# An attention and expert kernel: equal experts first, fewer fill products, other orders

## The chip, the core and the metric

The kernel runs on one core of a Trainium2 chip. A core has TensorE (PE, matrix products; PEld is its weight load), VectorE (DVE), ScalarE (ACT), GpSimd (POOL) and SyncE (SP), each with its own instruction stream, and 16 DMA engines that all of them share. The metric is the device time of one execution in microseconds; lower is better.

## The reference

The attention has 8 batches of 8 heads, 576 positions, 64 columns per head and 32 memory slots. phi is turned into weights by a softmax over the slots, and k and v are averaged with them to 32 rows per head; q then attends to these 32 rows.

```python
a = exp(phi - max(phi, axis=2)); a = a / (sum(a, axis=2) + 1e-09)
k_m = einsum('bhsm,bhsd->bhmd', a, k); v_m = einsum('bhsm,bhsd->bhmd', a, v)
attn = softmax(q @ k_m.T / sqrt(64));  x = attn @ v_m      # then [4608, 512]
y_dense = relu(x @ w1_dense) @ w2_dense
expert_idx = argmax(x @ w_gate, axis=1);  gate_w = softmax(x @ w_gate)[expert_idx]
y_moe[mask] = gate_w[mask, None] * (relu(x[mask] @ w1[e]) @ w2[e])   # for each expert e of 8
out = y_dense + y_moe
```

All is float32 outside; the hidden width is 512.

## The kernel before

The work is done batch by batch. A place in the order, 0 to 7, is not the batch's number: `seq` says which batch of the input stands at each place, and all names below use the place (`k` of batch 1 is that of the second place). For each batch the kernel picks one expert for all its rows from an estimate (`choose`, from the mean weights of v), loads that expert's two weight matrices, and keeps a flag; rows that would have needed another expert are handled at the end by a general path (`others`) behind a branch, which these inputs do not enter.

The steps of a batch, with their names in the order string: loads `Lphi`, `Lk`, `Lv`, `Lq`; `e0`, `e1` exponentials of phi (L352); `z`, `rz` their sums; `kv` (at place 0 apart as `kk` and `vv`) the sums over positions (L392), with `km` and `vm` after them; `T` (`Tk`, `Tv`) transposes of the means; `vTc`, `kTc` copies; `qT0`, `qT1` transposes of q on DVE; `s` scores (L503); `ET0`, `ET1` exponentials; `Z0`, `Z1` their sums (L536); `ln0`, `ln1`, `inv0`, `inv1` the reciprocals on ACT; `A0`, `A1` the attention (L565); `vg`, `vgc`, `pc`, `choose` the expert (L573 to L616); `L`, `mxeq`, `ex`, `gates` the gate of each row. The dense half folds v's means into w1_dense (`fd`, then copies `vd0`, `vd1`), takes four hidden products `hd0` to `hd3` (L741) with their relu `Hd`, and five output chunks `yd0` to `yd4` (L818; `yd4` is the half-size last one) written to `y` by `Yd`. The expert half is the same with `fe`, `ve`, `he`, `He`, `ye`, and `Ye` adds it to `y` with the row's gate (L853). The last place (`INNER`) multiplies the gate in at `He` and has one sum for both halves.

Loads. k, v, q and all weights are cast from float32 to float16 by GpSimd's DMA queue (L221, L249, L255, L259, L271, L276); phi goes there too (L204), but for the first batch's, which SP loads in halves (L213). `w1` and `w2` of a batch (L271, L276) need the chosen expert in a register of GpSimd, which its queue waits for at that point, with all later loads behind it. There are four places for expert weights (`NW`, `place_of`). At a place in `PAIRED`, the load carries a condition and is skipped when the expert is that of the batch before. Stores `o0`, `o1` (two chunks together) and `o4` (the last one, in two halves) are issued by SP (L859, L870).

Order. Everything is in one written order, `ORDER`, which is walked once by `go`; each engine takes its own steps in that order. `/A`, `/V`, `/P` picks ScalarE, VectorE or GpSimd for a step, and `+n` puts n fill products (L181) ahead of a step's own products: products of a matrix of ones into the PSUM tile that the step writes next, which compute nothing that is used. The tail is a branch on `any_i` at L1002 around the general path; the program's last instructions have line L1032.

```python
n, waits[0] = waits[0], 0
for _ in range(n):
    nc.tensor.matmul(p, lhsT=onesb, rhs=onesb[:, 0:1].to_broadcast([128, p.shape[1]]), start=True, stop=True)
```

Of the kernel before, what the change touches and what calls it, by code (L numbers as in the profile page):

```python
# [25 lines left out]
Yd3:0/V Lq:1 w2:0 yd0:0 fd:1 qT0:1 vgc:1 Yd0:0/A pc:1+7 Lphi:2/P kTc:1/V Lv:2 Lk:2 qT1:1 s:1+3  # L26
ye0:0+1 ET0:1 Lq:2 ET1:1 Lv:3 Z0:1 ln0:1 vd1:1/V inv0:1 Lq:3 vd0:1/V ye3:0 Z1:1 ye4:0 ln1:1 choose:1
Ye0:0 inv1:1 Lphi:4/P Ye3:0 A0:1 yd2:0 ye2:0 A1:1 Yd2:0/A hd1:1 ye1:0 hd3:1 Ye2:0 L:1 Ye1:0 w1:1
mxeq:1 e1:2 e0:2 Hd1:1/A ex:1 hd0:1 Ye4:0 Hd0:1/A z:2 fe:1 ve0:1/A Hd3:1/V ve1:1/A kv:2 hd2:1 rz:2
vm:2 km:2 qT0:2 T:2+5 vTc:2/A w2:1 fd:2 Hd2:1/A yd4:1 Lphi:3/P kTc:2/A qT1:2 vd1:2/A vg:2 vd0:2/V  # L30
vgc:2 s:2 Yd4:1/A ET0:2 yd3:1 pc:2 choose:2 gates:1 Z0:2 ET1:2 ln0:2 Yd3:1/V yd2:1 he1:1 inv0:2 A0:2
He1:1/A Z1:2 yd0:1 ln1:2 qT0:3 inv1:2 he0:1 He0:1/A Lk:3 A1:2 Yd0:1/V he2:1 yd1:1 He2:1/A he3:1
He3:1/A hd3:2 L:2 ye0:1 Hd3:2/V mxeq:2 hd0:2 e0:4 Yd2:1/V Ye0:1 Hd0:2/V e0:3 hd1:2 qT1:3 ex:2 e1:3
ye2:1 z:3 kv:3 Hd1:2/A Yd1:1/A hd2:2 ye1:1 rz:3 km:3 vm:3 Ye2:1 T:3 Ye1:1 e1:4 Hd2:2/A yd4:2 Yd4:2/V
kTc:3/A s:3 w1:2 ye4:1 vTc:3/A Ye4:1 ET1:3 fe:2 ve0:2/V vg:3 Lv:4 Lq:4 vgc:3 Lk:4 w2:2 Z1:3 ET0:3
ve1:2/A ye3:1 ln1:3 inv1:3 he3:2 He3:2/V Z0:3 ln0:3 pc:3 yd0:2 inv0:3 yd1:2 Yd0:2/A he1:2 yd2:2
Yd1:2/A He1:2/A A1:3 choose:3 Ye3:1 A0:3 he2:2 L:3 He2:2/A he0:2 gates:2 fd:3 ex:3 kv:4 mxeq:3 z:4
He0:2/V Yd2:2/A qT1:4 yd3:2 rz:4 km:4 vm:4 vd0:3/A vd1:3/A hd1:3 Hd1:3/A qT0:4 ye1:2 T:4 ye3:2
Yd3:2/A Ye1:2 kTc:4/A s:4 ET1:4 w1:3 vTc:4/A Ye3:2 ye0:2 Ye0:2 ET0:4 fe:3 vg:4 Z1:4 ln1:4 Z0:4 vgc:4
pc:4 ve1:3/V ln0:4 ye2:2 choose:4 Ye2:2 ve0:3/A hd0:3 hd2:3 Hd0:3/A Hd2:3/V ye4:2 fd:4 Lphi:5/P  # L40
inv1:4 inv0:4 hd3:3 Hd3:3/A Ye4:2 vd1:4/A he1:3 Lk:5 yd2:3 he0:3 vd0:4/V A0:4 Lv:5 yd3:3 He1:3/A
# [995 lines left out]
```

## Time and profile before

| | us |
|---|---|
| median of 3 runs | 171.67 (169.57 to 172.39) |
| the profiled execution | 169.97 |
| its span, first to last instruction | 168.3 |
| PE busy in it | 148.2 (88%) |
| DVE busy | 109.1 (65%) |
| ACT busy | 93.1 (55%) |
| POOL busy | 33.6 (20%) |

The span is shorter than the execution by what lies around it, 1.67 us. Busy times are shares of the span; fill products count as busy. A busy PE includes products at either clock. The DMA engines are shared, and their share of busy time is a mean over 16.

### The profile page before, as it was taken

The page shows a single profiled execution, that of the slowest core. Times are in us where ns is not written, and L with a number is a line of the kernel's source. Part 1 is how long each engine was busy: PE and PEld are TensorE (multiplying, and loading weights), DVE is VectorE, ACT ScalarE, POOL GpSimd, SP SyncE. Part 2 cuts the span into 40 slices and gives each one's busy share as a digit, 9 for nine tenths or more (in the row PEclk, how much of TensorE's full clock was granted, in tenths as well). Part 3 has the DMA queues.
Part 4 walks back from the last instruction along what each step waited for, and adds up shares of the span by engine and source line. Part 5 has one row for each costly group of instructions (what it writes and reads, how often), then busy time and mean ns, then how long its engine had stood idle before and what let it go on. Part 6 is the DMA issues. An engine that isn't in the chain of part 4 may idle for free.

```text
span 168.3 us, 5081 instructions
## 1 busy us (share of the span) xinstructions
PE 148.2 (88%) x2133; PEld 86.9 (52%) x2133; DVE 109.1 (65%) x296; ACT 93.1 (55%) x204; POOL 33.6 (20%) x56
## 2 busy tenths in 40 slices
PE   7964989988998999999899979999996999999910
...
DMA  4999807999999999999999999999999999679650
GB/s 119 185 201 236 218 7 90 205 208 257 232 208 207 299 248 208 208 214 161 229 210 206 248 241 208 179 196 223 208 200 201 320 357 345 195 291 383 244 167 9
DMA packets 22549, 36.06 MB, mean 214 GB/s; under 512 B 1268, under 2 KB 18676, under 8 KB 22520
## 3 DMA queue, kind: packets, MB, share of 16 engines
...
## 4 chain that ended last, share of the span: by engine, by line
PE 55%; DMA 27%; DVE 6%; issue 5%; POOLq 2%; ACT 1%; POOL 1%; DVEq 0%; ACTq 0%
PE p_y L818 28%; DMA W<-in_moe_w_dram 16%; DMA kv<-in_k_dram 11%; PE p_h L741 10%; PE p_kv L392 3%; PE p_att L181 2%; PE p_s L181 2%; PE p_vw L721 2%; PE p_s L503 2%; PE p_z L536 1%; POOLq L623 1%; PE p_att L643 1%; DVE qT L480 1%; PE p_kv L181 1%; DVE y L853 1%
## 5 line engine op out<-in xcount | busy, mean ns | idle before, releaser
L818 PE MATMUL p_y<-W,HTe 128*128 128x512 f16 (+1 forms) x192 | 37.2, 345 | 2.0 <-DMA W<-in_moe_w_dram 1.9
L818 PE MATMUL p_y<-w2d,HTd 128*128 128x512 f16 (+1 forms) x192 | 37.3, 345 | 0.0
L853 DVE SCALAR_TENSOR_TENSOR y<-p_y,gm,y 128x512 f32<-128x512 f32 (+1 forms) x35 | 23.9, 693 | 9.3 <-PE p_y L818 8.8
L271 POOL DMA_DIRECT2D W<-in_moe_w_dram x8 | 4.6, 572 | 97.2 <-DMA W<-in_moe_w_dram 23.1
L818 PEld LDWEIGHTS <-HTe 128*128 128x128 f16 (+1 forms) x192 | 15.0, 101 | 14.4 <-DMA W<-in_moe_w_dram 2.5
L781 ACT ACTIVATE HTd<-p_h 128x576 f16<-128x576 f32 x21 | 13.7, 651 | 13.0 <-PE p_h L741 11.0
L844 ACT ACTIVATE y<-p_y 128x512 f32<-128x512 f32 (+1 forms) x25 | 13.5, 555 | 13.2 <-PE p_y L818 13.2
L818 PEld LDWEIGHTS <-HTd 128*128 128x128 f16 (+1 forms) x192 | 14.9, 101 | 11.4 <-issue 1.1
L741 PE MATMUL p_h<-A,vwd 128*128 128x288 f16 x128 | 20.6, 287 | 0.3 <-ACT HTd L781 0.2
L741 PE MATMUL p_h<-A,vwe 128*128 128x288 f16 x128 | 20.0, 286 | 0.0
L518 ACT ACTIVATE ET<-p_s 128x256 f16<-128x256 f32 x32 | 10.7, 397 | 10.4 <-PE p_s L503 5.5
L741 PEld LDWEIGHTS <-vwe 128*128 128x128 f16 x128 | 12.0, 98 | 7.4 <-issue 0.7
L181 PEld LDWEIGHTS <-onesb 128*128 128x128 f16 x167 | 10.6, 111 | 9.2 <-issue 6.4
L741 PEld LDWEIGHTS <-vwd 128*128 128x128 f16 x128 | 11.3, 97 | 6.6 <-issue 1.6
L781 ACT ACTIVATE HTe<-p_h 128x576 f16<-128x576 f32 x18 | 11.6, 650 | 4.8 <-PE p_h L741 4.8
L565 DVE TENSOR_TENSOR A<-ET,lnz 128x576 f16<-128x576 f16 x16 | 11.6, 742 | 0.7 <-ACT lnz L558 0.7
L480 DVE STREAM_TRANSPOSE qT<-q 128x576 int32<-128x576 int32 x16 | 12.0, 763 | 0.0
L352 ACT ACTIVATE E<-phi 128x576 f16<-128x576 f32 x16 | 10.4, 680 | 2.7 <-DMA phi<-in_phi_dram 2.7
L549 ACT ACTIVATE lnz<-p_z 128x576 f32<-128x576 f32 x16 | 10.2, 656 | 2.1 <-PE p_z L536 2.1
L392 PE MATMUL p_kv<-kv,E 64*32 64x128 f16 (+1 forms) x648 | 7.5, 220 | 4.4 <-issue 2.5
L783 DVE TENSOR_SCALAR HTd<-p_h 128x576 f16<-128x576 f32 x11 | 8.3, 754 | 4.3 <-PE p_h L741 4.2
L846 DVE TENSOR_SCALAR y<-p_y 128x512 f32<-128x512 f32 (+1 forms) x15 | 9.4, 632 | 2.4 <-PE p_y L818 2.3
...
## 6 DMA issues: line engine op xcount, KB each, us to landing
...
```

Of the source, the lines that this page charges most:

```text
L181: nc.tensor.matmul(p, lhsT=onesb, rhs=onesb[:, 0:1].to_broadcast([128, p.shape[1]]), start=True, stop=True,)
L352: nc.scalar.activation(out=x["E"][:, :, hs].rearrange("p t j m -> p j t m"), in_=x["phi"][:, hs], func=AF.Exp,)
L392: nc.tensor.matmul(x["kvz"][a][M * j : M * j + M, Dh * u : Dh * (u + w)], lhsT=x["E"][rs, t, j], rhs=x["kv"][rs, u : u + w, j, t], start=( ...
L480: nc.vector.transpose(out=st[b]["qT"][:, js].rearrange("p j n u -> p (j n u)").bitcast(I32), in_=st[b]["q"][:, js].rearrange("p j t d -> p ...
L518: nc.scalar.activation(out=o.rearrange("m (g p k) -> m g p k", g=2, k=K2), in_=p_s[:, :, 0 : 2 * K2 * PB].rearrange("m g (k u p) -> m u g ...
L549: nc.scalar.activation(out=st[b]["lnz"][:, a].rearrange("p (h c) -> p h c", h=2), in_=st[b].pop(("pz", a))[:, :, 0:HC], func=AF.Ln,)
L565: eng.tensor_mul(out=st[b]["A"][:, a], in0=st[b]["ET"][:, a], in1=st[b]["lnz"][:, a])
L741: nc.tensor.matmul(p_h[:, h, 0:HC], lhsT=vw[:, g, 128 * ft : 128 * ft + 128], rhs=a[:, g, HC * h : HC * h + HC], start=(g == 0), stop=(g = ...
L781: nc.scalar.activation(out=o, in_=in_[:, :, 0:HC], func=AF.Relu)
L818: nc.tensor.matmul(p_y[n * u : n * u + n, 0:w], lhsT=HT[:, ft, at], rhs=w2[:, ft, w * u : w * u + w], start=(first and ft == 0), stop=(las ...
L844: nc.scalar.activation(out=o, in_=p_y, func=AF.Copy, scale=1.0 / SC)
L853: nc.vector.scalar_tensor_tensor(out=o, in0=p_y, scalar=x["gm"][:, c : c + 1], in1=o, op0=ALU.mult, op1=ALU.add)
```

## The change

Batches at places 0 and 1 are still batches 0 and 7 of the input; batches 2 and 6, which stood at places 6 and 7, come to places 2 and 3, so that `PAIRED` is (1, 3), and the last three places each load a weight place of their own. phi of the second batch is loaded by SP, whole (`Lphi:1` without `/P`). The fill products go from 167 to 88; those of `kk` and `vv` go to an unused part of the tile and are 384 columns wide, and none stands at `kv` of a later batch. A step `warm` takes the tile of the gate's product ahead of the fills (it has no fills of its own in the order). `cons8` is the second part of `cones`. The last batch's chunks 0 to 3 are stored one by one. The branch around the general path has a label with a hint, marked at `fin`, and the general path is its preferred fall-through block. The order is written anew.

```diff
 ORDER = """
-cones:0 cid:0 Lwg:0 wgt:0/V wgm:0+10 Lk:0 wgc:0 Lphi0:0 cblk:0 Lv:0 ciota:0 Lphi1:0 ciotac:0 e0:0
-Lq:0 e1:0 z:0+3 rz:0 kk:0+49 km:0 Tk:0+6 kTc:0/A vv:0+24 vm:0 Tv:0+12 vTc:0/A vg:0+17 qT1:0 qT0:0
-s:0+9 vgc:0 pc:0 Lw1d:0 ET0:0 ET1:0 Z0:0+3 ln0:0 Z1:0+1 choose:0 fd:0 ln1:0 Lphi:1/P inv0:0 inv1:0
-vd1:0/V A0:0 A1:0 vd0:0/A hd1:0+9 L:0 Lw2d:0 Hd1:0/V hd3:0 e0:1 e1:1 Hd3:0/A ex:0 hd0:0 w1:0 hd2:0
-Hd0:0/A fe:0 ve1:0/A Lv:1 Hd2:0/V Lk:1 ve0:0/A yd3:0+1 he1:0 He1:0/A he2:0 He2:0/V mxeq:0 he3:0+1
-yd1:0 He3:0/A z:1 he0:0 kv:1 yd4:0 He0:0/A Yd4:0/A gates:0 rz:1 vm:1 km:1 Yd1:0/V T:1+6 vTc:1/A vg:1
...
-Yd2:7/V o1:7 yd0:7 ye0:7 Yd0:7/A o0:7 pn:0 flags:0 yd4:7 ye4:7 Yd4:7/A o4:7
+Lphi0:0 e0:0 Lphi1:0 e1:0 ciota:0 cones:0 warm:0 ciotac:0 Lk:0 Lwg:0 cid:0 cons8:0 z:0+30 wgt:0/V
+rz:0 kk:0+1 km:0 cblk:0 wgm:0+12 Lq:0 qT1:0 Lv:0 Lw1d:0 Tk:0+2 Lphi:1 qT0:0 e1:1 kTc:0/V s:0+7 ET0:0
+ET1:0 vv:0+5 wgc:0 Z1:0+1 e0:1 Z0:0 vm:0 Tv:0 vTc:0/A fd:0+2 ln0:0 vg:0 Lk:1 ln1:0 inv1:0 A1:0
+inv0:0 vd0:0/A vd1:0/A A0:0 hd0:0+13 Hd0:0/A Lv:1 Lq:1 vgc:0 pc:0 hd2:0 Hd2:0/A choose:0 L:0 ex:0
+mxeq:0 gates:0 Lw2d:0 hd3:0+4 z:1 Hd3:0/A rz:1 kv:1 qT0:1 hd1:0+8 km:1 vm:1 qT1:1 T:1 vTc:1/V
+Hd1:0/A fd:1+2 kTc:1/V vg:1 s:1 yd1:0 vd1:1/A ET0:1 Z0:1+1 yd4:0 vd0:1/V ET1:1 Yd1:0/V w1:0 vgc:1
+ln0:1 Lphi:2/P Yd4:0/A fe:0 pc:1 Z1:1 ve1:0/V ve0:0/A yd2:0 ln1:1 choose:1 he0:0 He0:0/V Yd2:0/V
...
+yd0:5 Yd0:5/V o4:1 Yd2:5/A he3:5 He0:5/A he2:5 fd:6 inv0:6 He2:5/A yd4:5 A0:6 vd0:6/A He3:5/A
+vd1:6/V L:6 he1:5 gates:5 mxeq:6 Lv:7 ex:6 Yd4:5/A Lk:7 yd1:5 Yd1:5/V qT1:7 hd1:6 w2:5 w1:6 w2:6 z:7
...
+Hd2:6/V Ye3:5 hd3:6 Hd3:6/A T:7 ye2:5 vTc:7/V kTc:7/A vg:7 vgc:7 s:7 ye4:5 ET0:7 yd4:6 Ye2:5 pc:7
+Z0:7 Ye4:5 ET1:7 choose:7 ln0:7 Yd4:6/V inv0:7 ye0:5 Ye0:5 Z1:7 yd2:6 o1:0 fd:7 vd0:7/V he0:6 ln1:7
+inv1:7 he1:6 yd1:6 Yd2:6/A He1:6/A He0:6/A yd3:6 he2:6 o0:0 o4:2 o1:2 o0:1 o0:5 Yd1:6/A o0:2 he3:6
+yd0:6 o4:0 vd1:7/V He2:6/A A0:7 Yd0:6/A He3:6/V A1:7 ye2:6 o1:5 o4:5 hd1:7 Hd1:7/A Yd3:6/A gates:6
+Ye2:6 w1:7 hd2:7 w2:7 Hd2:7/A ye1:6 Ye1:6 L:7 hd0:7 ex:7 ye4:6 mxeq:7 fe:7 Ye4:6 ve0:7/A o0:3 o1:1
+Hd0:7/A hd3:7 Hd3:7/A ye0:6 ye3:6 gates:7 pg:7 ve1:7/V gB:7/A yd1:7 Ye3:6 Ye0:6 he2:7 he1:7 He2:7
+He1:7 yd0:7 he0:7 He0:7 he3:7 yd3:7 He3:7 ye3:7 Yd3:7/V ye1:7 o0:6 pn:0 o1:6 o0:4 ye0:7 yd2:7 o4:6
+o3:7 Yd0:7/V o0:7 ye2:7 Yd1:7/V Yd2:7/A o1:7 o2:7 yd4:7 ye4:7 flags:0 fin:0 Yd4:7/A o4:7
 """
...
-    seq = [0, 7, 1, 3, 4, 5, 2, 6]
-    place_of = [0, 0, 1, 2, 3, 0, 1, 1]
+    seq = [0, 7, 2, 6, 1, 3, 4, 5]
+    place_of = [0, 0, 1, 1, 2, 3, 0, 1]
     NW = 4
-    PAIRED = (1, B - 1)
+    PAIRED = (1, 3)
...
+    @step("warm")
+    def _(b, i, e):
+        st[0]["pw"] = one.tile([128, 512], F32, tag="one", name="p_w")
+        fill(st[0]["pw"][:, 0:32])
...
-        fill(x["kvz"][0][:, Dh * u : Dh * (u + w)])
+        if not b:
+            fill(x["kvz"][0][:, 2 * Dh :])
...
-    @step(*(f"o{c}" for c in range(NP)))
+    @step(*(f"o{c}" for c in range(NCH - 1)))
     def _(b, c, e):
-        nc.sync.dma_start(
-            out=rows_out(b, c), in_=st[b]["y"][:, 2 * D * c : 2 * D * c + 2 * D]
-        )
+        if b == B - 1:
+            rows_c = rows_out(b, c // 2)[:, :, D * (c % 2) : D * (c % 2) + D]
+            nc.sync.dma_start(out=rows_c, in_=st[b]["y"][:, D * c : D * c + D])
+        elif c < NP:
+            nc.sync.dma_start(
+                out=rows_out(b, c), in_=st[b]["y"][:, 2 * D * c : 2 * D * c + 2 * D]
+            )
...
+    @step("fin")
+    def _(b, i, e):
+        tc.mark_branch_hint_location("redo", 0, engs)
...
-    with tc.If(anyv > 0, preferred_fallthrough_block=False):
+    with tc.If(anyv > 0, preferred_fallthrough_block=True, label="redo"):
```

GpSimd's queue in the new order is: iota, k, identity, q, v of batch 0, w1d, k, v, q of batch 1, w2d, w1:0, phi and k of 2, w2:0, v of 2, w1:1, q of 2 and 3, phi, k, v of 3, w2:1, w1:2, and so on to v and k of 7, w2:5, w1:6, w2:6, w1:7, w2:7. SP's is phi of batch 0 in halves, the gate, phi of batch 1, and then the stores, o4:3 and o1:4 first. Before, the first stores were o4:5 and o1:4.

## Rows read from the trace of the kernel before

**Rows 1.** The span in 40 equal slices, busy tenths of each.
```profile
PE   7964989988998999999899979999996999999910
...
DMA  4999807999999999999999999999999999679650
```

**Rows 2.** Stretches: us, busy us and (count) per engine, PEclk, DMA share, GB/s.
```profile
0.00:45.06 45.06, 37.08 (x599) 20.85 (x599) 19.01 (x62) 16.61 (x37) 14.25 (x25) 0.89 0.93 177
45.06:160.40 115.34, 111.07 (x1536) 66.09 (x1535) 90.12 (x235) 76.12 (x167) 19.30 (x31) 1.00 1.07 237
...
1.90:20.20 18.30, 13.79 (x300) 9.29 (x299) 5.22 (x18) 2.25 (x5) 4.53 (x7) 0.76 1.10 218
20.20:25.90 5.70, 4.91 (x59) 2.00 (x58) 0.97 (x5) 2.58 (x9) 0.65 (x1) 0.87 0.06 12
```

**Rows 3.** Fill products alone: busy in a stretch; two of their runs, timeline.
```profile
0.00:45.06 45.06, 20.44 (x162) 10.25 (x162) 0.89 0.93 177
...
1.18 4.01 PE L181 MATMUL p_w<-onesb 128*128 128x512 f16 x10 [1.18 <-DVE ones L289]
...
25.47 2.13 PE L181 MATMUL p_h<-onesb 128*128 128x512 f16 x9
```

**Rows 4.** The chain that ended last, 1 to 27 us: start, us, what.
```profile
1.61 8.20 DMA kv<-in_k_dram
...
13.30 2.48 issue
...
22.34 0.41 PE p_s L503 x24
...
25.25 0.75 POOL W L271
```

**Rows 5.** Timeline of GpSimd: start, us, instruction [idle before <-releaser].
```profile
5.86 0.57 POOL L259 DMA_DIRECT2D w2d<-in_moe_w_dense_dram  x1
25.25 0.75 POOL L271 DMA_DIRECT2D W<-in_moe_w_dram  x1 [18.82 <-issue]
...
45.56 0.05 POOL L271 DMA_DIRECT2D W<-in_moe_w_dram  x1 [4.77 <-DMA W<-in_moe_w_dram]
```

**Rows 6.** Timeline of TensorE: the first hidden product of batch 0.
```profile
27.63 0.81 PE L741 MATMUL p_h<-A,vwd 128*128 128x288 f16 x4
```

**Rows 7.** The chain, 44 to 55 us: TensorE's steps back to back.
```profile
44.02 0.86 PE p_y L818 x4
44.88 0.24 PE p_z L536 x2
...
48.87 0.49 PE p_h L741 x4
...
50.93 0.34 PE p_vw L721 x8
51.27 0.67 PE p_kv L392 x72
...
54.59 0.40 PE p_s L503 x21
```

**Rows 8.** Waits of TensorE: total us, times, longest us.
```profile
PE p_y L818 <- DMA W<-in_moe_w_dram: 1.9, 2, 1.0
...
PE p_vw L721 <- DMA W<-in_moe_w_dram: 1.7, 3, 0.7
```

**Rows 9.** Line L271, the w1 loads: from issue to landing.
```profile
DMA to landing us min/median/max: 5.7/7.5/8.5
```

**Rows 10.** All loads of expert weights: from issue to landing.
```profile
DMA to landing us min/median/max: 5.7/9.2/19.7
```

**Rows 11.** Line L1002, TensorE's sequencer: ns min/median/max, first and last start.
```profile
L1002 PEldq COMPARE_BRANCH  x2: 89/2103/4117, 161.1 to 161.5; - x2
```

**Rows 12.** Line L1032, GpSimd's sequencer at the end.
```profile
L1032 POOLq DRAIN  x3: 46/106/1687, 165.8 to 168.0; - x3
```

**Rows 13.** Timeline of SP: the last store.
```profile
160.81 1.14 SPq L870 DMA_DIRECT2D out_dram<-y  x2
```

More of the change, by code (lines that the diff above doesn't have):

```diff
@@ L25 @@
-yd1:0 He3:0/A z:1 he0:0 kv:1 yd4:0 He0:0/A Yd4:0/A gates:0 rz:1 vm:1 km:1 Yd1:0/V T:1+6 vTc:1/A vg:1
[L26 to L41, printed above, removed]
@@ L42 @@
-Yd2:3/A He0:3/A A1:4 L:4 gates:3 mxeq:4 he2:3 ex:4 he3:3 yd0:3 e0:5 e1:5 yd1:3 z:5 He2:3/V Yd0:3/V
-hd1:4 Lq:5 qT1:5 qT0:5 rz:5 He3:3/A Yd1:3/A Yd3:3/A kv:5 yd4:3 w1:4 km:5 vm:5 Hd1:4/A fe:4 w2:3
-hd2:4 T:5 Yd4:3/V ve1:4/A hd0:4 ye1:3 ve0:4/A Hd2:4/V kTc:5/V gates:4 vTc:5/A Hd0:4/A vg:5 s:5 ye4:3
-ye0:3 ET1:5 Ye4:3 hd3:4 ye2:3 ET0:5 Z0:5 Ye0:3 Lphi:6/P Lq:6 Hd3:4/A ln0:5 vgc:5 pc:5 Z1:5 ln1:5
-Ye1:3 inv1:5 Ye2:3 ye3:3 Ye3:3 choose:5 qT1:6 A1:5 he2:4 yd3:4 inv0:5 A0:5 he0:4 He0:4/A yd2:4 e0:6
-yd0:4 Lk:6 Lv:6 he1:4 Yd0:4/V He2:4/A e1:6 L:5 He1:4/V he3:4 yd1:4 Yd3:4/A ex:5 Yd2:4/V qT0:6
@@ L48 @@
-Yd1:4/A fd:5 kv:6 vd0:5/A w2:4 mxeq:5 He3:4/V yd4:4 ye4:4 vd1:5/A hd1:5 z:6 Hd1:5/A Yd4:4/A ye2:4
-gates:5 rz:6 km:6 vm:6 hd0:5 Hd0:5/A w1:5 Ye2:4 Lphi:7/P ye0:4 hd2:5 T:6 vTc:6/A Ye4:4 hd3:5 Hd2:5/V
-kTc:6/A Hd3:5/A ye3:4 e1:7 s:6 ET1:6 Ye0:4 vg:6 Ye3:4 fe:5 Lq:7 Lv:7 ve0:5/A ET0:6 ve1:5/V ye1:4
-Ye1:4 qT0:7 fd:6 he0:5 vgc:6 Z0:6 yd2:5 pc:6 vd0:6/A He0:5/A ln0:6 Z1:6 yd3:5 he3:5 vd1:6/V inv0:6
-ln1:6 inv1:6 yd0:5 He3:5/A choose:6 Yd0:5/A A0:6 qT1:7 A1:6 Lk:7 Yd2:5/V he1:5 w2:5 he2:5 yd1:5 L:6
```

41 lines of the change are left out of this document (30 added, 11 removed).

## The prediction

> **What bounds the kernel now.** I read the span in 40 slices first, then the busy time of stretches, the chain that ended last, GpSimd's own order, and the end. The slices show two engines that share the bound: TensorE at 9 tenths nearly throughout, and the DMA engines at 9 from the eighth slice to the thirty-fourth, with a hole at the sixth [rows 1]. TensorE's row hides a difference. Up to 45.06 us it is busy 37.08 us, but 20.44 of these are fill products that compute nothing; from there to its last product at 160.4 it is busy 111.07 of 115.34 us [rows 2, 3]. So the later part is close to a bare sum of products, and the loose time lies at the start.
>
> The chain says why the start is loose. k of the first batch lands at 9.81 us, TensorE sits 2.48 us on nothing that the profile shows at 13.30, the scores of batch 0 end at 22.75, and only at 25.25 does GpSimd issue the first expert weight [rows 4]. GpSimd's order explains the hole: its issue before that was w2d at 5.86; then it sat 18.82 us at the head of w1:0, with k, v and q of the second batch queued behind [rows 5]. From 20.20 to 25.90 the DMA engines are 0.06 busy and move 12 GB/s, against 218 before that. TensorE's granted clock was 0.76 of full on average from 1.90 to 20.20, a mix of its two levels of 2.4 and 1.2 GHz [rows 2].
>
> **The change, part by part.** I follow the new order to a point where its work can be compared with the old one's.
>
> Loads. In the new order k, v, q of batch 1 and w2d stand ahead of w1:0, and phi of batch 1 goes to SP, so the wait for the choice no longer empties the DMA engines. Up to and with w1:0 there are phi 576, k, q, v 3 x 576, w1d and w2d 2 x 512, the gate's 16, phi of batch 1 576, its k, v, q 3 x 576 and w1:0 512 KB (sizes from the shapes): 6,160 KB or 6.31 MB. At 218 GB/s from 1.90 that is 28.9 us, so 30.8; a landing is told up to 2 us after its last byte (an estimate: the old w1:0, on idle engines, took 5.7 us [rows 9] where its bytes need 2.4 and its issue 0.75): 32.8.
>
> phi by SP stands beside k of batch 0. It delays k by 0 to 2.7 us (576 KB at 218 GB/s, all of it ahead of k). I take 1.1, in the lower half, because k's issue also moves ahead of the identity and the fills ahead of z last to 9.6 anyway. The Trainium skill ("DMA: Bandwidth & Descriptors", section "Queues, rings and completion order") says that each DMA engine takes turns, a packet at a time, between the queues that have work: a transfer moved to SP's queue is then no extra bandwidth but a share taken from k. By that rule the delay would be the full 2.7 us and the sum 1.6 us worse; no row here shows the two side by side.
>
> Start of TensorE. The 30 fills ahead of z: ten took 4.01 us from 1.18 on, at the lower clock, nine at full clock 2.13 us, so 0.22 each [rows 3]: they end near 9.6. k's sums run from 10.9 to 11.7; 12 fills and the gate's product to 14.7; Tk with 2 fills to 15.2; 7 fills and the scores to 17.1. Before, the scores ended at 22.75 [rows 4]: the half-clock stretch goes, and the scores no longer stand behind v's sums. From the scores to the first hidden product (27.63 [rows 6]) the old kernel needs 4.9 us of exponentials, logarithms and copies. The new order adds e0 of batch 1, the copy of vT and the second vd on ScalarE, 1.5 us (an estimate: that stretch has some eight such steps in 4.9). So the first hidden product is at 23.5. The 2.48 us at 13.30 falls into the sums of v; with 79 fills fewer it may go, moves, or stays, and at most 1 us of it reaches the hidden product: I take 0.
>
> From 23.5 to fe:0 TensorE has hd x4 (0.49 each), L and s (0.40 each), kv 0.67, T and fd (0.34 each, as the fold), yd1 0.86, yd4 half of that, Z0 0.24, 0.6 for pc, z, vg, and 15 fills (3.3) [rows 7]: 9.2 us with 1 us of the steps between, hence 33 us. w1:0 (32.8) is just there. pc:0 now stands behind hd0:0, so the choice and w1:0's issue come 1 to 1.5 us later than 25.25; that is covered as long as k, v, q and w2d are still moving, to about 28.
>
> At 45.06 the old kernel has also done fe:0, he x4, yd3, yd0, ye0 and ye3 of batch 0, pc:1 and Z1:1: 0.34 + 4 x 0.49 + 4 x 0.86 + 0.1 + 0.24 = 6.1 us [rows 7]; all else that it has done the new one has done by fe:0. So the new one is there at 39.2: **5.8 us ahead**. If w1:0 lands 2 us late the lead is 3.8; if k isn't delayed and ScalarE's chain is no longer than before, 7.8.
>
> The middle. The 111.07 us of products stay, and 4.27 us of gaps; 3.6 of waits for expert weights are on record, nearly all here [rows 8]. With both pairs first, batches 0 to 3 need two experts and not three, so 1,024 KB (4.8 us at 218 GB/s) leave the first half. But TensorE is ahead too: by the same sum w2:0 lands near 40.6 for a use at 40.4, w1 of batch 2 near 59.5 for a use at 60. I credit 1.5 us (bounds 0 and 3.6).
>
> The late expert. The load at the last position was skipped, as the one at 45.56 was (0.05 us of issue [rows 5]), and is now real. Between pc:7 and fe:7 TensorE has 7 chunks, 7 hidden products, Z0, Z1, fd, L and a last chunk: 6.0 + 3.4 + 0.5 + 0.3 + 0.4 + 0.4 = 11.1 us [rows 7]. From pc to the issue it was 2.5 us at batch 0 [rows 4], so 8.6 are left. The w1 loads landed 5.7 to 8.5 us after issue [rows 9], any weight up to 19.7 [rows 10]. TensorE takes its work in order, so hd3, ye0, ye3 and all that is behind fe:7 waits with it. I charge 1.0 (0 by rows 9, 11.1 by the end of rows 10).
>
> The stores. Chunks of the last batch go singly, four issues in place of two; o4 is issued at the last y as before, and the single o2 ahead of it ends 0.3 us before that: 0, at most 0.6 (half of the 1.14 that SP takes for o4's two [rows 13]).
>
> The end. After the last y SP issues o4 at 160.81 [rows 13]. Meanwhile TensorE's branch around the general path takes 4.117 us, from 161.5 [rows 11], and GpSimd's drain of 1.687 us begins only at 165.8, after it [rows 12]. If the hint brings the code behind the branch in time, GpSimd drains while the store lands and the end comes up to 1.7 us earlier; the store sets the rest. Bounds 0 and 1.7; I take 1.2.
>
> **Sum** on the profiled execution (span 168.3, 169.97 with what lies around it): 169.97 - 5.8 - 1.5 + 1.0 - 1.2 = 162.5. That execution is 1.7 below the median of the runs shown; for a median I add half of it: **163.3 us**.
>
> **The rivals.**
> Faster still, 160.2: the weights that leave the first half take all 3.6 us of waits away (2.1 more) and the late expert is covered (1.0). For it: weights are the main gaps after 45 us. Against: the two ties above.
> No change, 169.6: the loads bind and the lead is given back, so only the end's 1.2 us is left. For it: DMA slices 8 to 34 are full, so a TensorE that is early waits for k and v. Against: the 5.7 us hole is DMA time, and the loads get it back too.
> Slower, 173.4: w1:7 lands 19.7 us after issue, because stores of some 3 MB that SP has released by then move beside it, and fe:7 waits 11.1 us with TensorE's queue behind it (163.3 - 1.0 + 11.1). It decides from a landing of 8.6 us on, one for one, and from 18 us on the change is a loss. For it: the largest w1 landing is at the edge already. Against: no w1 landing came near 18.
> The change doesn't do what it says: the hint has no effect, 164.5. That a pair isn't skipped gets no chance: both pairs are skipped now, at other positions.
>
> **How the numbers follow.** Forecast 0.53 and the hint without effect 0.07, together with a range of their own from 160.8 to 166.5 (lead 3.8 to 7.8, end 0 to 1.7); faster still 0.13; no change 0.19; slower 0.08. About 2%, 168.2 to 175.1, is what a measurement of this kernel can tell from no change. Below lie the first three: 0.73. Above lies the worse half of the slower case: 0.05. The rest, 0.22, is the same. The range for 8 in 10 goes from 159 to 170: it takes in the faster case and most of the unchanged one.
>
> **What would show it.** Right: no hole in the DMA slices, scores of batch 0 near 17 us, fe:0 near 33, ye3:0 and Z1:1 done near 39, TensorE's branch under 1 us. Wrong: TensorE idle between 24 and 45 for k, v or w1:0; over 3 us at fe:7; landings of k, v and weights lengthened by stores from 112 us on; a clock below full after 12 us; from last product to end still 7.9 us.

## The result, and the profile after

The changed kernel took 161.11 us at the median of four runs (160.71 to 164.83) beside 170.79 us for the kernel before on the same chip (4 runs, 169.57 to 172.39): a ratio of 0.9448 [0.9345, 0.9551]. The profile taken with it is of the 164.83 us run, the longest of the four, so the rows below are of a second submission of the same kernel (the run `again`, whose profiled execution took 159.97 us, the shortest of its four, with a span of 158.2). The old kernel's profile is of an execution with a mean granted clock of 0.960, where that of `b_hint`, in the same order, had 0.983; what this does to the start is told there. Line numbers are 8 to 18 higher than before from L329 on: L741 is now L750, L1002 is L1020, L1032 is L1050.

The span in 40 slices, second profile of the changed kernel, against [rows 1]:

```profile
PE   6969999999998999998999999998999999999960
...
DMA  5999999999999999999999999999999987999962
```

The hole at the sixth DMA slice is gone, and TensorE is at 8 or 9 tenths from the fourth slice to the thirty-eighth. The same in stretches, cut where a comparable point lies, against [rows 2] (columns: span, busy us and count of PE, PEld, DVE, ACT, POOL, then PEclk, DMA share, GB/s):

```profile
0.00:41.20 41.20, 38.43 (x540) 20.21 (x541) 19.65 (x66) 19.06 (x41) 12.65 (x25) 1.00 1.09 204
41.20:152.75 111.55, 109.61 (x1517) 64.73 (x1514) 86.05 (x230) 76.88 (x166) 19.86 (x31) 1.00 1.09 241
```

Behind the start TensorE is busy 109.61 of 111.55 us: gaps of 1.94 us in place of 4.27. The start, from TensorE's timeline, against [rows 3, 4, 6]:

```profile
11.69 0.74 PE L401 MATMUL p_kv<-kv,E 64*32 64x64 f16 x72 [1.19 <-DMA kv<-in_k_dram]
...
17.38 0.49 PE L512 MATMUL p_s<-qT,kT 32*32 32x288 f16 x32
...
24.08 0.65 PE L750 MATMUL p_h<-A,vwd 128*128 128x288 f16 x4
...
32.09 0.48 PE L512 MATMUL p_s<-qT,kT 32*32 32x288 f16 x32
...
34.61 0.41 PE L730 MATMUL p_vw<-W,vT 64*32 64x512 f16 x8
...
42.74 1.89 PE L827 MATMUL p_y<-W,HTe 128*128 128x512 f16 x8
```

k's sums are at 11.69, the scores of batch 0 at 17.38 (22.34 before), the first hidden product at 24.08 (27.63 before), fe:0 at 34.61, with no wait for its weight. In the old kernel the point to compare with, 45.06 in [rows 2], is where ye3:0 and Z1:1 are done and ye4:0 begins:

```profile
45.06 0.63 PE L818 MATMUL p_y<-W,HTe 128*64 128x256 f16 x8
```

The last row above holds ye3:0 and ye1:0, so ye3:0 ends near 43.6. By then this kernel has also done yd2 of batch 0 (0.86), three hidden products (3 x 0.49) and L (0.40) of batch 1, 2.73 us that the old one had not done at 45.06: a comparable point of 40.9, a lead of 4.2 us on these two executions.

GpSimd's timeline, against [rows 5]; the first row is the last load ahead of the choice, then w1:0, the skipped w1:1, and w1:7:

```profile
7.42 0.60 POOL L259 DMA_DIRECT2D w2d<-in_moe_w_dense_dram  x1
27.10 0.74 POOL L271 DMA_DIRECT2D W<-in_moe_w_dram  x1 [19.08 <-DVE at L682]
...
38.28 0.05 POOL L271 DMA_DIRECT2D W<-in_moe_w_dram  x1 [7.66 <-DMA W<-in_moe_w_dram]
...
130.30 0.74 POOL L271 DMA_DIRECT2D W<-in_moe_w_dram  x1 [16.98 <-DVE y L862]
```

GpSimd still sits 19 us at the head of w1:0, but k, v and q of batch 1 and w2d are now issued ahead of that wait. Of TensorE's waits the only one for a load, against [rows 8], and then the time from issue to landing of the w1 loads, against [rows 9]:

```profile
PE p_kv L401 <- DMA kv<-in_k_dram: 1.2, 1, 1.2
```
```profile
DMA to landing us min/median/max: 6.9/7.3/8.7
```

No expert weight is among the waits (1.9 and 1.7 us before). fe:7 came at 139.67, 9.4 us after the issue of its weight, with no wait. That is this execution: those of `a_pairstores` and `a_nohint`, in the same order up to the end, wait 0.5 and 0.8 us for expert weights, the 164.83 us run 2.1. In that run w1:7 landed late, k came 0.6 us later, and TensorE's granted clock was 0.83 in 10 to 20 us; three rows of its TensorE timeline:

```profile
12.28 0.78 PE L401 MATMUL p_kv<-kv,E 64*32 64x64 f16 x72 [1.84 <-DMA kv<-in_k_dram]
12.99 4.13 PE L181 MATMUL p_w<-onesb 128*128 128x512 f16 x12
...
144.46 0.41 PE L730 MATMUL p_vw<-W,vT 64*32 64x512 f16 x8 [1.58 <-DMA W<-in_moe_w_dram]
```

The 12 fill products at 12.99 took 4.13 us; in `again` they took 2.79. The end, second profile: TensorE's branch, GpSimd's drains (ns min/median/max, first and last start) and the last store, against [rows 11 to 13]:

```profile
L1020 PEldq COMPARE_BRANCH  x1: 404/404/404, 153.2 to 153.2; - x1
```
```profile
L1050 POOLq DRAIN  x3: 46/97/1538, 154.1 to 157.9; - x3
```
```profile
153.19 1.15 SPq L883 DMA_DIRECT2D out_dram<-y  x2
```

The branch fell from 4.117 to 0.404 us, the long drain lies under the store, and last product to end of span is 152.73 to 158.2, 5.5 us, where it was 7.9.

So on two profiled executions 10.1 us of span went: 4.2 at the start, 2.4 at the end, and 3.5 between (from the comparable point to the last product 115.34 before, 152.73 - 40.9 = 111.8 now). The medians lie 8.5 (`again`) to 9.7 us apart; how much of the 4.2 belongs to the two executions and not to the kernels is seen at `b_hint`.

### The profile page after: what moved, and what is told of

It is laid out like the page before. It is cut to its first block, busy times and chain, and to the rows that moved or that the text cites. A ratio compares the mean times of both kernels' runs of the same rounds, so it can differ in the third digit from the quotient of the medians.

```text
span 163.1 us, 4917 instructions
## 1 busy us (share of the span) xinstructions
PE 149.6 (92%) x2054; PEld 85.5 (52%) x2054; DVE 105.9 (65%) x294; ACT 96.5 (59%) x206; POOL 32.5 (20%) x55
## 5 line engine op out<-in xcount | busy, mean ns | idle before, releaser
L790 ACT ACTIVATE HTd<-p_h 128x576 f16<-128x576 f32 x28 | 18.0, 653 | 11.8 <-PE p_h L750 10.8
L271 POOL DMA_DIRECT2D W<-in_moe_w_dram x8 | 4.6, 572 | 88.9 <-DVE at L682 21.0
L827 PEld LDWEIGHTS <-HTe 128*128 128x128 f16 (+1 forms) x192 | 14.9, 101 | 12.3 <-issue 1.7
L750 PE MATMUL p_h<-A,vwd 128*128 128x288 f16 x128 | 19.9, 286 | 0.0
L750 PE MATMUL p_h<-A,vwe 128*128 128x288 f16 x128 | 19.8, 286 | 0.0
L853 ACT ACTIVATE y<-p_y 128x512 f32<-128x512 f32 (+1 forms) x21 | 11.3, 536 | 10.6 <-PE p_y L827 10.4
L360 ACT ACTIVATE E<-phi 128x576 f16<-128x576 f32 x16 | 11.1, 692 | 9.4 <-DMA phi<-in_phi_dram 9.4
L790 ACT ACTIVATE HTe<-p_h 128x576 f16<-128x576 f32 x22 | 14.1, 656 | 3.9 <-PE p_h L750 3.8
L750 PEld LDWEIGHTS <-vwe 128*128 128x128 f16 x128 | 12.1, 98 | 7.0 <-issue 0.5
L855 DVE TENSOR_SCALAR y<-p_y 128x512 f32<-128x512 f32 (+1 forms) x19 | 12.4, 657 | 4.4 <-PE p_y L827 4.1
L181 PEld LDWEIGHTS <-onesb 128*128 128x128 f16 x88 | 8.8, 107 | 12.1 <-issue 4.8
L750 PEld LDWEIGHTS <-vwd 128*128 128x128 f16 x128 | 11.6, 97 | 6.3 <-issue 1.4
L567 ACT ACTIVATE lnz<-lnz 128x576 f32<-128x576 f32 x16 | 10.6, 681 | 0.3
L558 ACT ACTIVATE lnz<-p_z 128x576 f32<-128x576 f32 x16 | 10.2, 649 | 0.7 <-PE p_z L545 0.6
L181 PE MATMUL p_att<-onesb 128*128 128x512 f16 (+1 forms) x32 | 9.2, 451 | 1.3 <-DVE onesb L288 1.3
## 6 DMA issues: line engine op xcount, KB each, us to landing
W<-in_moe_w_dram POOLq DMA_DIRECT2D x16, 512.0 KB, 10.9
kv<-in_k_dram POOLq DMA_DIRECT2D x8, 576.0 KB, 10.5
```

The costliest lines, as they stand in the source:

```text
L360: nc.scalar.activation(out=x["E"][:, :, hs].rearrange("p t j m -> p j t m"), in_=x["phi"][:, hs], func=AF.Exp,)
L567: nc.scalar.activation(out=lnz, in_=lnz, func=AF.Exp, scale=-1.0)
L750: nc.tensor.matmul(p_h[:, h, 0:HC], lhsT=vw[:, g, 128 * ft : 128 * ft + 128], rhs=a[:, g, HC * h : HC * h + HC], start=(g == 0), stop=(g = ...
L790: nc.scalar.activation(out=o, in_=in_[:, :, 0:HC], func=AF.Relu)
L827: nc.tensor.matmul(p_y[n * u : n * u + n, 0:w], lhsT=HT[:, ft, at], rhs=w2[:, ft, w * u : w * u + w], start=(first and ft == 0), stop=(las ...
L853: nc.scalar.activation(out=o, in_=p_y, func=AF.Copy, scale=1.0 / SC)
```

## The experiments

**again: the changed kernel once more.**

> The changed kernel once more, for a profile of an ordinary run. Its profile on record is of a run of 164.8 us; the other three runs lie at 160.7 to 161.2. Theory A (the lead is made at the start by loads that aren't held up): here fe:0 starts 2 to 3 us sooner than the 36.6 us of the profile on record, and the last product ends near 154. Theory B (the 3.7 us between the runs arise at the wait for the last expert's first weight): fe:0 is again near 36.5 and the wait at fe:7 is gone. Time 161 by both.

160.35 us at the median of four (159.97 to 161.2), ratio 0.9545 [0.9473, 0.9617]. Each theory had a part: fe:0 came 2.0 us sooner than in the 164.83 us run (34.61 for 36.60), and the wait of 1.58 us at fe:7 is gone. 160.35 is the number that the variants of the changed kernel are held against below. The chip was not the same for all: the kernel before took 168.89 us on that of `again`, `b_hint`, `b_loads` and `a_oldpairs`, 170.21 on that of `a_loads`, `a_nofill`, `a_phi_pool` and `b_newpairs`, 169.54 on that of `a_nohint`, `a_pairstores` and `cand1`, and 168.94 on that of `cand2`, so up to 1.3 us of a difference to `again` can be the chip. The ratios are to the kernel before on the same chip.

**b_hint: the kernel before with the hint alone.**

```diff
-    with tc.If(anyv > 0, preferred_fallthrough_block=False):
+    with tc.If(anyv > 0, preferred_fallthrough_block=True, label="redo"):
```

(and the step `fin` ahead of the last `Yd4:7`)

> The kernel before with the hint and the fall-through block alone. Theory: the end, from last product to end of span, goes from 7.9 to 5.5 us, TensorE's branch from 4.1 to 0.4 us, and the time falls by 1.7 to 2.4 us (ratio 0.986 to 0.990). Rival (the last store sets the end, the shorter end of the changed kernel comes from its order): ratio 0.998 to 1.002.

166.74 us (four runs, 164.09 to 169.41) against 168.89, so 2.15 us less, without an interval. Last product to end fell from 7.9 to 6.3 us (158.30 to 164.6). TensorE's branch and GpSimd's drains of this kernel:

```profile
L1007 PEldq COMPARE_BRANCH  x1: 404/404/404, 159.0 to 159.0; - x1
```
```profile
L1037 POOLq DRAIN  x3: 46/97/1620, 160.0 to 164.3; - x3
```

The drains start 1.7 us after the last product, where it was 5.4 [rows 12]. A small edit, and about a fifth of the whole gain. It has two parts, the hint and the preferred fall-through block, and no run here separates them.

This profile shows something else. Its span is 3.7 us shorter than the old kernel's, and 1.6 us at the end are not all of it: the same row as at 45.06 before comes 2.4 us earlier, in an order that is the same up to there:

```profile
42.69 0.63 PE L818 MATMUL p_y<-W,HTe 128*64 128x256 f16 x8
```

The first hidden product is as much earlier (25.12 for 27.63). So the start of the old order moves by 2.4 us from one execution to another, and held against this one the changed kernel's lead at the start is 1.8 us, not 4.2.

**a_nohint: the changed kernel without the hint.**

```diff
-    with tc.If(anyv > 0, preferred_fallthrough_block=True, label="redo"):
+    with tc.If(anyv > 0, preferred_fallthrough_block=False):
```

(and the hint at `fin` taken out)

> The changed kernel with the old form of the branch around the general path (no label, no hint, the general path not preferred as fall-through). Theory (the hint alone carries the end): TensorE's branch takes about 4 us again, GpSimd's last drain starts behind it, last product to end of span goes from 5.5 back to 7.5 to 8 us, and the time rises by 2 to 2.5 us, about 162.5 to 163. Rival (the single stores or the new order of the end shortened it, and the hint only moves idle time): within 0.7 us of the changed kernel, about 160.5 to 161.5.

162.92 us (six runs, 160.81 to 165.41), ratio 0.965 [0.9537, 0.9763]: 2.6 us above `again`. Last product to end: 154.10 to 161.4, 7.3 us. Its branch and drain:

```profile
L1020 PEldq COMPARE_BRANCH  x2: 89/1906/3722, 154.5 to 155.0; - x2
```
```profile
L1050 POOLq DRAIN  x3: 46/106/1602, 159.0 to 161.1; - x3
```

The branch is back at 3.7 us and the drain begins behind it. Both directions agree: the hint with its block order is worth some 2 us in either kernel.

**a_pairstores: chunks 0 to 3 of the last batch stored in pairs.**

```diff
-        if b == B - 1:
+        if False:
...
-o3:7 Yd0:7/V o0:7 ye2:7 Yd1:7/V Yd2:7/A o1:7 o2:7 yd4:7 ye4:7 flags:0 fin:0 Yd4:7/A o4:7
+Yd0:7/V ye2:7 Yd1:7/V o0:7 Yd2:7/A o1:7 yd4:7 ye4:7 flags:0 fin:0 Yd4:7/A o4:7
```

> The changed kernel with chunks 0 to 3 of the last batch stored in pairs again, as before. Theory (the single stores cost and bring nothing, since o4 at the last y sets the end): within 0.6 us of the changed kernel, about 160.2 to 161.5. Rival (the single stores let the last data leave earlier, so that o4 lands on emptier queues): 0.7 to 1.5 us longer, about 161.5 to 162.5.

162.07 us (four runs, 161.12 to 162.46), ratio 0.9655 [0.9563, 0.9747]. The intervals overlap, but the profile says where a difference is: the last product is at 152.76, as in `again`, and the end at 159.4, 1.2 us later. From the last 8.5 us of the two kernels, the issues of o4 with the median us from issue to landing, with single stores and then with pairs:

```profile
out_dram<-y SPq DMA_DIRECT2D x2, 64.0 KB, 3.6
```
```profile
out_dram<-y SPq DMA_DIRECT2D x2, 64.0 KB, 4.5
```

o4 is issued at the same time (153.19 and 153.22), its issue takes 1.59 in place of 1.15 us, and it lands 0.9 us later behind a last pair of 512 KB. The rival was right, and the forecast's "0, at most 0.6" for the stores had the wrong sign.

**b_loads: the kernel before with the loads of batch 1 ahead of w1:0.**

```diff
-... ex:0 hd0:0 w1:0 hd2:0
+... ex:0 hd0:0 Lv:1 Lk:1 Lq:1 w1:0 hd2:0
```

(and the three taken from their old places)

> The kernel before with the loads of v, k and q of the second batch ahead of w1:0 in GpSimd's queue, nothing else. Theory (the 5.7 us in which the DMA engines stand idle are the main loss at the start): kv:1 no longer waits for k at 36.6, and the time falls by 2 to 5 us. Rival (the start is bound by ScalarE's and TensorE's own chain, the order of PE must change with the loads to use them): less than 1 us, since TensorE still takes its steps in the old order, fe:0 and he ahead of z:1, and w1:0 now lands some 8 us later behind three loads: up to 3 us slower.

170.42 us (five runs, 170.04 to 175.43), ratio 1.0115 [1.003, 1.02]: slower by 1.2%. w1:0 was issued at 25.49 (25.25 before), but then had to share the engines, and the old order has the expert next. TensorE's timeline, of the longest of its five executions (175.43 us), the only one profiled:

```profile
34.29 0.63 PE L721 MATMUL p_vw<-W,vT 64*32 64x512 f16 x8 [3.23 <-DMA W<-in_moe_w_dram]
...
36.96 2.13 PE L741 MATMUL p_h<-A,vwe 128*128 128x288 f16 x8
...
41.60 0.80 PE L392 MATMUL p_kv<-kv,E 64*32 64x128 f16 x72
```

The loaded k and v aren't used until 41.60. Filling the hole alone brings nothing (that is in the ratio; the size of the wait is of the longest execution), so the forecast's reason for the lead was half of one.

**a_loads: the changed kernel with w1:0 ahead of the loads of batch 1.**

```diff
-... Hd0:0/A Lv:1 Lq:1 vgc:0 pc:0 hd2:0 Hd2:0/A choose:0 L:0 ...
+... Hd0:0/A vgc:0 pc:0 hd2:0 Hd2:0/A choose:0 w1:0 Lk:1 Lv:1 Lq:1 L:0 ...
```

(and `Lk:1` and `w1:0` taken from their old places)

> The changed kernel with one edit to GpSimd's queue: w1 of batch 0 goes back ahead of k, v and q of batch 1 (right behind the choice), so that GpSimd's queue waits for the choice with them behind it, as in the kernel before. Theory (the early loads carry the lead of the new order's start): k, v and q of batch 1 then land 5 to 9 us later than in the changed kernel, while TensorE needs z, kv and s of batch 1 ahead of the first expert's products; the DMA engines show a hole before w1:0 and the time is 4 to 8 us longer, about 164.5 to 168.5. Rival (the lead comes from the start of TensorE and ScalarE alone, and the load of w1 of batch 0, coming earlier, makes up for the rest): within 1.5 us of the changed kernel, about 160 to 162.

172.68 us (four runs, 172.07 to 174.01), ratio 1.0135 [1.0062, 1.0209]: 12.3 us above `again`, more than the theory's 4 to 8. w1:0 in GpSimd's order (its issue before that is w1d, at 4.49), TensorE's sums of batch 1, and the stretch of the hole:

```profile
26.85 0.74 POOL L271 DMA_DIRECT2D W<-in_moe_w_dram  x1 [21.60 <-DVE at L682]
```
```profile
38.39 1.16 PE L401 MATMUL p_kv<-kv,E 64*32 64x128 f16 x72 [11.14 <-DMA kv<-in_v_dram]
```
```profile
19.00:26.80 7.80, 7.77 (x89) 4.27 (x77) 3.53 (x15) 5.60 (x13) 0.00 (x0) 1.00 0.02 4
```

7.8 us with the DMA engines 0.02 busy, then an 11.14 us wait, because in the new order batch 1 stands ahead of the first expert; and behind the wait the 72 sums take 1.16 us, where `again` needs 0.80. `b_loads` and this run say one thing from two sides: the queue and TensorE's order are one edit. Either order in the other's queue is no faster than the old kernel.

**a_phi_pool: phi of batch 1 back on GpSimd's queue.**

```diff
-... Tk:0+2 Lphi:1 qT0:0 ...
+... Tk:0+2 Lphi:1/P qT0:0 ...
```

> The changed kernel with phi of batch 1 moved back from SP's queue to GpSimd's, at the same place in the order. Theory (phi on SP's queue delays k of batch 0, by a share of the engines, as the prediction charged with 1.1 of at most 2.7 us): k lands 0.5 to 2.7 us earlier than the changed kernel's, and the scores with it; but phi of batch 1 then lands after q, v and w1d, near 17 to 20 us, and its exponentials stand ahead of those of the scores on ScalarE, so 0 to 3 us of that is given back: between 1.5 us faster and 1.5 us slower, about 159 to 162. Rival (phi on SP costs nothing, since k's own landing is set by the queue's first descriptors): k lands within 0.3 us of the changed kernel's and the late exponentials alone remain: 1 to 3 us slower, about 161.5 to 163.5.

165.12 us (four runs, 163.62 to 166.13), ratio 0.9657 [0.9554, 0.9759]: 4.8 us above `again`, some 3.5 without what the chip can give; both theories were too mild. k's sums, the fill ahead of Z, and the exponential of phi on ScalarE:

```profile
10.86 0.75 PE L401 MATMUL p_kv<-kv,E 64*32 64x64 f16 x72
...
22.28 0.38 PE L181 MATMUL p_z<-onesb 128*128 128x512 f16 x1 [3.65 <-ACT ET L533]
```
```profile
20.89 0.68 ACT L360 ACTIVATE E<-phi 128x576 f16<-128x576 f32 x1 [15.63 <-DMA phi<-in_phi_dram]
```

k's sums are 0.83 us earlier (10.86 for 11.69), and no longer wait for k: TensorE has only just done its fills and z. k itself gained more. Its load from issue to landing, in `again` and here (both issued at 1.60):

```profile
DMA to landing us min/median/max: 10.0/10.0/10.0
```
```profile
DMA to landing us min/median/max: 8.6/8.6/8.6
```

So phi on SP costs k 1.4 us, of which the fills hide 0.6. But on GpSimd's queue phi lands behind q, v and w1d at 20.9, and the exponentials of the scores, behind it on ScalarE, come at 21.48: the first hidden product moves to 28.84. The charge of 1.1 us for phi on SP had about the right size (1.4 at k, 0.83 at its sums); what it bought was not in the sum. The Trainium skill ("DMA: Bandwidth & Descriptors", section "Queues, rings and completion order") has each engine take turns between queues, which by the forecast's reading would cost k the full 2.7 us; the 1.4 us measured here is about half of that.

**a_nofill: no fill products at all.**

```diff
-... z:0+30 ... kk:0+1 ... wgm:0+12 ... Tk:0+2 ... s:0+7 ... hd0:0+13 ... hd1:0+8 ...
+... z:0 ... kk:0 ... wgm:0 ... Tk:0 ... s:0 ... hd0:0 ... hd1:0 ...
```

> The changed kernel without any of its fill products (all counts in the order at zero; nothing that is used is left out). Theory (the fills that are left hold the clock at the start): without them TensorE's granted clock is at the lower level for much of the first 25 us and the steps of batch 0 take up to twice as long: 1 to 4 us longer, about 161.5 to 164.5. Rival (the fills are idle filling, and the 26 us of the start are set by loads and by ScalarE): within 0.7 us of the changed kernel. A second rival (fills stand ahead of steps that are late, so they cost): 0.5 to 2 us faster, about 158.5 to 160.

161.15 us (four runs, 160.57 to 162.33), ratio 0.9493 [0.9416, 0.9569]: no difference that can be measured from 160.35 or 161.11. TensorE's timeline of that kernel:

```profile
16.20 0.71 PE L512 MATMUL p_s<-qT,kT 32*32 32x288 f16 x32 [3.08 <-DVE kT L127]
...
23.44 1.12 PE L750 MATMUL p_h<-A,vwd 128*128 128x288 f16 x4 [2.60 <-DVE vg L594]
...
28.34 0.66 PE L750 MATMUL p_h<-A,vwd 128*128 128x288 f16 x4
...
33.92 0.41 PE L730 MATMUL p_vw<-W,vT 64*32 64x512 f16 x8 [0.46 <-DMA W<-in_moe_w_dram]
```

Without fills four hidden products take 1.12 in place of 0.65 us until 28 us, so the fills do keep the pace. But they also stand in the way: without them the scores come at 16.20 (17.38), the first hidden product at 23.44 (24.08), and fe:0 at 33.92 (34.61), where it waits for its weight. TensorE is less busy by 17.1 us (148.05 less 130.93; the 88 fills took 22.9, and other products got slower), and that buys nothing net.

**a_oldpairs: the changed kernel with the old `seq`, `place_of` and `PAIRED`.**

```diff
-    seq = [0, 7, 2, 6, 1, 3, 4, 5]
-    place_of = [0, 0, 1, 1, 2, 3, 0, 1]
-    PAIRED = (1, 3)
+    seq = [0, 7, 1, 3, 4, 5, 2, 6]
+    place_of = [0, 0, 1, 2, 3, 0, 1, 1]
+    PAIRED = (1, B - 1)
```

> The changed kernel with the batches in their old places (seq, place_of and PAIRED as before): w1 and w2 at place 3 are real loads, those at place 7 are skipped. Theory of the prediction (fewer weights in the first half take waits away, the late expert costs 1 us): 0.5 to 3 us slower than the changed kernel. Rival 1 (the late expert is the dearer side): the wait at fe:7 of 1.6 us and more goes, 1 to 3 us faster. Rival 2 (both cancel): within 0.5 us.

175.05 us (four runs, 173.84 to 176.53), ratio 1.0431 [1.0342, 1.0519], 14.7 us above `again`: far outside all that was expected. TensorE's waits, and, from the chain that ended last, the hidden products behind fe:3 (start, us, what):

```profile
PE p_y L827 <- DMA W<-in_moe_w_dram: 6.3, 2, 5.8
PE p_vw L730 <- DMA W<-in_moe_w_dram: 3.9, 1, 3.9
```
```profile
79.92 2.03 PE p_h L750 x8
```

The weights of place 3 are now real, and the new order issues them just ahead of their use, since they were to be skipped there. There are 10.2 us of waits, and behind the 3.9 us one eight hidden products take 2.03 us, where they take 0.98 at full clock. The rest of the 14.7 us was not followed. This says that the order is written around the pair. It doesn't price the pair.

**b_newpairs: the kernel before with the new `seq`, `place_of` and `PAIRED`** (the same three lines, the other way round).

> The kernel before in its old order, with the new sequence of batches, places of weights and PAIRED alone (so the skip moves from place 7 to place 3). Theory (the pairs pay only in an order written for them): the load at place 7 becomes real, and in the old order fe:7 stands a few us behind pc:7, so its weight is exposed by 2 to 6 us, against at most 3.6 us of weight waits that the skip at place 3 can take away: 0 to 4 us slower than before, about 171 to 175, with a wait for a weight at fe:7 in TensorE's rows. Rival (the pairs alone pay): the 1,024 KB that leave the first half take weight waits away at once and the last weight stays covered: 2 to 4 us faster, about 167 to 169. A third way, no effect within 1 us, would say that neither the early nor the late weight sets anything in the old order.

172.11 us (ten runs, 170.43 to 174.55), ratio 1.0114 [1.006, 1.0168]: 1.9 us slower, as the theory had it. TensorE at fe:7, and the stretch behind it, of the longest of the ten executions (174.55 us), the only one profiled:

```profile
146.98 0.63 PE L721 MATMUL p_vw<-W,vT 64*32 64x512 f16 x8 [4.38 <-DMA W<-in_moe_w_dram]
147.54 1.89 PE L818 MATMUL p_y<-W,HTe 128*128 128x512 f16 x4
```
```profile
147.00:154.00 7.00, 7.00 (x34) 3.22 (x34) 2.86 (x11) 1.24 (x2) 0.00 (x0) 0.59 0.97 357
```

This is the forecast's rival "slower" in small: the weight of the last place, issued at 139.02, is exposed by 4.38 us, and the clock is at 0.59 for the 7 us behind. How much of the 1.9 us at the median comes from this wait isn't shown, since no shorter execution was profiled. In the new order the same load was issued 9.4 us ahead of its use and was covered.

**cand1: chunks in place of fills.** Could the start be shorter still? 15 fills out, and yd1, yd4, yd2 of batch 0 ahead of the first expert.

```diff
-... hd3:0+4 z:1 Hd3:0/A rz:1 kv:1 qT0:1 hd1:0+8 km:1 vm:1 qT1:1 T:1 vTc:1/V
-Hd1:0/A fd:1+2 kTc:1/V vg:1 s:1 yd1:0 vd1:1/A ET0:1 Z0:1+1 yd4:0 ...
+... hd3:0 z:1 Hd3:0/A rz:1 kv:1 km:1 vm:1 hd1:0 qT0:1 Hd1:0/A T:1 vTc:1/A qT1:1
+kTc:1/A yd1:0 fd:1 vg:1 Yd1:0/A yd4:0 s:1 Yd4:0/A yd2:0 vd1:1/A ET0:1 Z0:1 ...
```

> The changed kernel with 15 fill products fewer (those at hd3 and hd1 of batch 0, fd and Z0 of batch 1) and a new order between 25 and 36 us: the means of k and v of batch 1 stand ahead of q's transposes on VectorE, and the dense chunks yd1, yd4 and yd2 of batch 0 stand ahead of the scores and the first expert fold, where the changed kernel had fills. Theory (the first expert weight lands near 34 us, tied to the choice near 27 us, and TensorE has real chunks that can be done while it waits): fe of batch 0 stays near 34 us, but with yd2 (0.86 us) done ahead of it and 3.3 us of fills gone, so 0.9 to 2 us faster than the changed kernel, about 158.5 to 160. Rival (the stretch after 35 us is set by loads that are already back to back, so that work done earlier only waits later): within 0.7 us, about 160 to 161.5. Second rival (without the fills products run at half pace, 1.1 us in place of 0.65 for four hidden products, as in the run without fills): 0.5 to 1.5 us slower.

164.82 us (six runs, 162.32 to 166.38), ratio 0.9729 [0.958, 0.9877]: 4.5 us above `again`. No theory named the cause:

```profile
32.85 1.87 PE L827 MATMUL p_y<-w2d,HTd 128*128 128x512 f16 x4 [3.22 <-DMA w2d<-in_moe_w_dense_dram]
```

w2d, last of the loads ahead of w1:0, lands at 32.8; in `again` it lands at 31.7, and yd1 stands at 32.51, behind it.

**cand2: `cand1` with w2d ahead of q of batch 1 as well.**

```diff
-... Lv:1 Lq:1 vgc:0 pc:0 ...
+... Lv:1 Lw2d:0 Lq:1 vgc:0 pc:0 ...
...
+... yd2:0 Yd2:0/A yd3:0 Yd3:0/A s:1 ...
```

> The run before this one with one more edit: w2d stands ahead of q of batch 1 in GpSimd's queue, and the dense chunks yd1, yd4, yd2 and yd3 of batch 0 stand ahead of the scores of batch 1. Theory (the start is bound by the order in which 6.3 MB land, and w2d was merely in the wrong place for early chunks): w2d lands near 29 us in place of 32.8, the 3.2 us wait of the run before is gone, four chunks are done by 33 us, q lands near 32, the scores and fe of batch 0 come near 34: 0.5 to 2 us faster than the changed kernel, about 158.5 to 160. Rival (the two halves of the load are worth the same, whichever comes first): the wait for w2d turns into a wait for q, ahead of the scores, and batch 1 stands behind it; the chunks that filled the time between the expert's hidden products are used up: equal to the changed kernel or up to 3 us slower, about 160.5 to 163.5.

164.01 us (six runs, 161.17 to 164.94), ratio 0.9728 [0.9666, 0.979]: the rival's way, half a us beyond its range. yd1 is at 29.41 without a wait, but the scores of batch 1 come at 34.36 (32.09), and TensorE then waits for their exponentials, where `again` had chunks left to do. Its TensorE timeline, of an execution of 161.17 us, the shortest of its six:

```profile
29.41 1.03 PE L827 MATMUL p_y<-w2d,HTd 128*128 128x512 f16 x4
...
34.36 0.48 PE L512 MATMUL p_s<-qT,kT 32*32 32x288 f16 x32
35.78 0.41 PE L545 MATMUL p_z<-ET,blk 128*128 128x288 f16 x2 [0.95 <-ACT ET L533]
```

Even so it is 1.2 us above that of `again`. Whichever half of the loads comes first, batch 0 or batch 1 stands late. No version tried was measurably faster than the changed kernel.

## Why the prediction was right, and where it wasn't

Sign, size and range held: 163.3 us forecast (159 to 170), 161.11 and 160.35 measured. The two numbers lie nearer to the rival "faster still" at 160.2, and step by step the sum was right in part by luck: it gave the start too much and the middle and the end too little.

- **The lead at the start, 5.8 us forecast, 4.2 measured against the old profile, 1.8 against the start of `b_hint`.** k's sums (10.9 forecast, 11.69), the scores' end (17.1, 17.8) and the first hidden product (23.5, 24.08) were each up to 0.8 late. The other 1.0 is a slip in the sum: from the first hidden product to fe:0 its own terms add to 9.5 us, not 9.2, and with the 1 us of the steps between to 10.5, which is what `again` took (24.08 to 34.61). w1:0 was late as well: issued at 27.10 where "1 to 1.5 us later than 25.25" was said, it landed 7.3 us later, at 34.4, and not at 32.8. The bytes were rightly counted: to 6.31 MB the DMA engines stayed full. The reason given, that the hole is refilled, holds only with TensorE's new order behind it (`b_loads`, `a_loads`). That the old start itself moves by 2.4 us between executions was not in the sum, which took one execution for the kernel.
- **"The half-clock stretch goes", by fewer and wider fills.** In `again` it went from 5.5 us on: 1.00 in the windows up to 41 us, where it was 0.76 from 1.90 to 20.20 [rows 2]. (In the first 5.5 us the fills are still at the lower pace, 0.43 us each and 0.22 after; the column doesn't show that, as the last section says.) In the 164.83 us run some of it was there again. But the clock wasn't worth anything by itself: without any fill the time is the same (`a_nofill`). What sets the start is when the loads land. The chain that ended last in `again` comes there from q of batch 1, 5.3 of the 6.3 MB, and from 6.68 to 29.22 us it is nothing but that landing:

```profile
6.68 22.54 DMA q<-in_q_dram
```
- **The middle, 1.5 us credited, and 1.0 charged for the late expert: 0.5 net, 3.5 measured.** This is the step that was mis-sized most, and the rival's mechanism took its place: in `again` all weight waits went, and w1:7 was covered. "8.6 left" for w1:7 was nearly right (9.4 from issue to fe:7), and the landing, at most 8.7 us, fits under it; in the 164.83 us run it took 10.87 and 1.58 us showed, in `a_nohint` 0.8 us at fe:7. Charging 1.0 was too much for some executions and too little for another. How much of the 3.5 the pairs alone bring was not settled: both runs that move them (`a_oldpairs`, `b_newpairs`) also break the fit between order and skip.
- **The stores, 0 forecast, 0.6 to 1.2 us gained** (last product to end 6.6 us in `a_pairstores` and 5.5 in `again`; without the hint 7.9 before and 7.3 in `a_nohint`). I asked when o4 is issued, and that is unchanged; it lands later behind a pair of 512 KB than behind single chunks of 256.
- **The end, 1.2 us for the hint, measured 1.6 to 1.8** between last product and end (7.9 to 6.3, 7.3 to 5.5) and 2.15 to 2.6 in the medians. The mechanism was as told: the drain no longer waits for the branch and lies under the store. Of the bounds 0 and 1.7 the upper one came true, not the 1.2 between. With the stores the whole end gained 2.4.
- **"No change" (0.19)** is out: the loads did bind in the start, but the lead wasn't given back, since gaps behind it fell too. **"Slower" (0.08)** showed itself only in the old order (`b_newpairs`).

The sum on spans was 7.5 us, and 10.1 were measured: 1.6 short at the start, 3.0 more in the middle, 1.2 more at the end. Against the start and the middle of `b_hint`'s execution the measured sum is 1.8 + 3.8 + 2.4 = 8.0 us, nearer to the 8.5 to 9.7 between the medians; the lead is then 4.0 short.
